# An adaLN block with linear attention and a SiLU MLP: EPS on ACT, mod products over four row tiles, other PSUM banks, engine orders drawn anew

## The chip, the cores and the metric

The kernel runs on one core of one Trainium2 chip. The metric is the device time of one execution in microseconds; the time of a kernel is the median of its timed runs. One further execution was taken by the hardware profiler, and all rows of the profile come from that one. TensorE is called PE here, VectorE DVE, ScalarE ACT, GpSimd POOL, and SP is the engine that issues most DMAs. L681 is line 681 of the kernel.

## The reference, cut to what matters

Sequence 2048, width D = 576, 32 heads of 18, hidden width F = 4608, all in fp32.

```
mod = (silu(c) @ w_mod).reshape(1, 6, 1, 576)
sa, ca, ga, sb, cb, gb = (mod[:, i] for i in range(6))
h = layernorm(x) * (1 + ca) + sa
q, k, v = heads(h @ wqkv);  phi(t) = where(t > 0, t + 1, exp(t)) + 1e-6
kv  = einsum("bhsd,bhse->bhde", phi(k), v);  z = einsum("bhsd->bhd", phi(k))
num = einsum("bhqd,bhde->bhqe", phi(q), kv)
den = einsum("bhqd,bhd->bhq", phi(q), z)[..., None] + 1e-6
x = x + ga * (merge(num / den) @ wo)
h = layernorm(x) * (1 + cb) + sb
x = x + gb * (silu(h @ w1) @ w2)
```

## The kernel before

**Arithmetic.** Each fp32 operand of a large product is split into a high part of type float32r and a low part that holds the rest (ACT copies the high part, DVE or POOL subtracts it: L118 and L311 for the low parts, L313 for the low part of a last chunk of 64 rows), and three products hi·hi, hi·lo and lo·hi are added in PSUM. So ACT and DVE have an eviction and a split to do for nearly everything that PE makes.

**Stages.** Tokens stand in 16 row tiles of 128, in four blocks of 512. First comes the start (0 to about 35 us): the column sums of the modulation for the first LayerNorm, statistics of the first four tiles (L175, L176), normalised tiles turned by PE (L383), modulated (L198) and split (hT, L118), and the first two k projections by passes (L400), each evicted by phi (L322 on ACT, L327 and L328 on DVE). Between those passes PE runs small products of constants that keep it occupied ("warm-ups", L405). Then a loop over t = 0 to 15 makes for each row tile a k projection (tile of PSUM psK), a v projection with its copies into vx, the kv product of the tile before (kv_mm, three PSUM tiles kvp0 to kvp2 that accumulate over all tiles) and one or two q projections. Between t = 5 and t = 8 the loop also makes the other four rows of the modulation: mod_piece (weights times silu(c), L511 and L513 on DVE, which wait for loads of w_mod), mod_row (L527, a row broadcast to all partitions, copied by ACT in L528) and mod_col (L520, columns for the second LayerNorm, copied by DVE in L522).

Then the masked kv matrix times wo is made per chunk (L706, split by L306 and L311/L313), beside q_norm of the first tiles. q_norm (L676 to L688) takes phi(q)·z, reduces it per head (L680), adds EPS (L681), inverts (L683) and multiplies (L684 on POOL); it then issues the load of x for the residual (L687, SP). The attention steps follow: s from 0 to 17 with three phases a step, q_norm of tile s, transposes of tile s − 1 (L738, with qT as the split result), the output product of tile s − 2 (L223 with qT, added in L752) and its LayerNorm statistics. Between the phases stand the late q projections (their PSUM comes from `big`, not psK), the turning of the second LayerNorm's tiles (L196, L211) and MLP group 0, made in the plain way (L812 up, L814 silu, L823 down, L828 add); its weights come by L768 and L770 (times gb) and are split in L771 and the line behind.

The other MLP groups (units, from about 380 us) use a scheme with seven products in place of eight per block: sums of blocks of h and of the weights (POOL's L955, L957, L960 and L1066, DVE's L933; sums of h go to DRAM and are streamed back into `room`), split by ACT (L936, L992, L1010) and DVE, up products L1248 with evictions (L1223 copies one to p, L1264, L1267) and down products L1321, added by DVE in L1329.

**PSUM.** The first pool holds kvp0 to kvp2 (a bank each), psK (two tiles of two banks) and psT (a bank). It is released after the loop and the M products; the second pool has three `big` tiles of two banks and two `small` ones of a bank. The pools give out banks in the order in which tiles are first asked for: before the change kvp0 to kvp2 are banks 0 to 2, psK 3 to 6 and psT 7, and `big` then covers 0-1, 2-3 and 4-5.

**Order.** Five engines have a fixed order for all that is issued before the first two units are done (about 405 us): the dictionary ORDERS holds for PE, DVE, ACT, POOL and SP a list of positions, and arrange (L104) chains the instructions of each engine in that order. An instruction thus waits for all that stands ahead of it on its engine, whatever it needs itself. What follows (units[2:], L1481) stands in program order on each engine and is interleaved by written-out plans.

The lines that the change touches outside the tables are the warm-ups' tile and the psT tile (L419 to L424 and L443), the modulation at t = 5 and 8 (L625 to L632) and L681.

Of the kernel before, what the change touches and what calls it, by code (L numbers as in the profile page):

```python
# [11 lines left out]
AF = mybir.ActivationFunctionType  # L12
# [6 lines left out]
EPS = 1e-6  # L19
# [3 lines left out]
def kernel(ctx: ExitStack, tc, A_x, A_wqkv, A_wo, B_x, B_w1, B_w2, c, w_mod, out):  # L23
# [28 lines left out]
    def f32(ap):  # L52
# [4 lines left out]
            0-107 114-116 108-110 117 111-113 118-2761  # L57
        """,
        "DVE": """
            1-2 0 6 4-5 11 7 12 8 13-14 9 18 15-16 10 17 19-20 29 21-22 24 23 25 28 26-27 30 45 31 46 32 34-35 37-38  # L60
            36 39-40 43 33 41-42 49 44 47-48 52 50-51 64 3 65 53-54 67 55 90 59 57 68 89 66 60 86 61 82 58 87 69 83
            88 62-63 84 70 150 73 71 74 72 75-76 91 78 77 56 80 85 81 93 79 94 92 151 95 152-153 99 98 100 96 154 97
            101-105 155 106-107 109 108 110-113 127-128 130 129 131 133-134 132 114 136 135 137-139 115 140-141 116
            143 117 144 142 118-126 145-149 156 184-186 157 187 160 188 161 225 189 162 158 224 164 159 163 228
            226-227 165 167 166 168-169 171 170 172-173 175 174 194-195 197 196 198-201 203-204 202 205-206 176
            207-208 210 177-179 209 211 180-183 190-193 212-216 218 217 219-220 222 221 223 229-230 232 231 233-261
            265 263 267-268 264 266 262 271-273 277-279 270 274-275 269 276 284 280-281 302 285 301 286 293 282
            294-295 305-307 287 303 314 288 315 289-291 283 304 316 324 292 325 296-299 326 308 300 333 309 334
            310-312 335 317 343 318 344 319-322 345 355 323 356 328-331 313 327 357 367 336 332 337 368 338-341 369
            376 342 377 348-349 346 350 353 351-352 347 378 387-388 358 354 359-366 389 406-407 370-371 375 408 425  # L70
            372-373 426 379-380 384 374 381-382 385 383 392 427 390 386 393 434 395 400 396-397 399 394 402 398 412
            435 413-414 403 415 391 416 422 411 417 421 420 418-419 401 436 405 428 423 409 424 410 429-432 404 433
            437-440 442-443 441 444-451 456 452-455 458-460 457 461-462 466 464 463 465 475 477 467 474 480 468-469
            482 478 471 486 483 473 472 489 470 488 496 495 494 479 484 476 497 491 485 490 498 481 487 506 499 501
            500 502 492 504 493 503 505 511 540 512 514 507-510 522 521 513 525 517 515-516 518-520 529 538 534
            523-524 526-527 539 528 531-532 530 533 535-537 542 541 543-546
        """,
        "Activation": """
            0-2 4-5 3 6-9 11 10 15 12 17 13-14 16 19 24 18 25 22 20 23 27 21 26 29 28 56 31 33 30 35 53 36-37 57 40
            34 54-55 38 41-42 39 48 32 43 49 51-52 50 58 44 46 59 47 45 60 62-65 67 66 61 68-72 74-75 73 76 79 77 80  # L80
            78 81-82 92 90-91 83-84 93 85-89 94-99 101-103 106 104 107 105 100 108-111 113-114 112 115 118 116 119
            117 120 131 121 129 132 130 122-128 133-136 138-139 137 140 143 141 144 142 145-147 149-150 148 151 154
# [13 lines left out]
        """,  # L96
        "SP": """
            0-27 31 34 28 30 32 35 33 29 42 36-37 43-46 51-53 38-41 54-57 59 58 60 47-50 67 66 65 61-62 68 63-64
            69-73 76 74-75 77-79 86 82 80-81 88 84 83 89 87 85 90-91 93 92 94 96 95 110 109 97 108 98-99 102 100
            103-104 101 105-107 114 111-113  # L100
        """,
    }
# [1414 lines left out]
```

## Time and profile before

| what | value |
|---|---|
| median of three timed runs | 1158.06 us (1158.06, 1159.26, 1156.38) |
| profiled execution | 1155.35 us, of which the span 1153.4 us |
| mean granted clock of PE | 0.996 |
| busy: PE / DVE / ACT / POOL | 1137.2 / 981.1 / 531.9 / 644.5 us |
| PE idle in the span | 16.2 us |
| DMA | 268.60 MB, 233 GB/s over the span |

The span is what the profiler's records cover; the 1.95 us beside it are start and end of the execution. A view of stretches gives the busy time of each engine in each stretch of the span and the clock that PE was granted, 1.00 being full speed. The view of waits sums how long an engine was idle ahead of an instruction, and names what ended the idleness. A timeline row has start, duration, engine, line, result and operands, and in brackets the idle time before it with what ended it. A releaser is inferred: what stands in brackets came last, not necessarily alone.

### The profile page before, as it was taken

What the parts mean: (1) busy time and instruction counts of PE and PEld (TensorE: products, weight loads), DVE (VectorE), ACT (ScalarE), POOL (GpSimd) and SP (SyncE); (2) the same over time, 40 slices, a digit from 0 to 9 for tenths busy, and PEclk for the clock granted to TensorE, in tenths of its full rate; (3) what the DMA queues carried; (4) which work ended last, traced back from release to release, by engine and by line L of the source; (5) the groups of instructions that cost most, each with busy time, mean ns of one, the idle gap of its engine ahead of it and who ended that gap; (6) DMA issues with size and microseconds to landing.
All of it is one profiled execution on the core that took longest, in us unless ns stands there. A gap on an engine that the chain in (4) does not pass through costs nothing.

```text
span 1153.4 us, 19610 instructions
## 1 busy us (share of the span) xinstructions
PE 1137.2 (99%) x7227; PEld 1056.4 (92%) x7227; DVE 981.1 (85%) x1554; ACT 531.9 (46%) x1085; POOL 644.5 (56%) x742
## 2 busy tenths in 40 slices
PE   8999999999999999999999999999999999999998
PEld 8999999899998899999999999999999999999998
DVE  6965644587788889998999999999999999999996
ACT  5643442436656544444444454454444444444541
POOL 1100000354533675777677667757767776776686
PEclk8999999999999999999999999999999999999999
DMA  9522100123158868769779769678697797697684
GB/s 288 155 82 78 42 1 1 45 72 124 33 230 311 311 262 332 300 249 349 275 260 355 276 255 360 267 295 326 261 340 291 256 349 277 256 356 277 254 311 154
DMA packets 58478, 268.60 MB, mean 233 GB/s; under 512 B 5580, under 2 KB 21712, under 8 KB 35344
## 3 DMA queue, kind: packets, MB, share of 16 engines
q1 hardware_dynamic: 58372, 267.36, 62.9%
q8 instruction: 57, 0.93, 0.3%
q14 instruction: 37, 0.30, 0.1%
q10 hardware_dynamic: 12, 0.00, 0.0%
HBM read 250.56 MB, written 16.78 MB: 232 GB/s over the span
## 4 chain that ended last, share of the span: by engine, by line
PE 92%; DVE 4%; DMA 2%; ACT 1%; issue 1%; POOL 1%; SPq 0%; DVEq 0%; ACTq 0%; POOLq 0%
PE up L1248 33%; PE down L1321 31%; PE psK L223 12%; PE big L223 5%; PE big L823 2%; PE small L812 2%; PE kvp L562 2%; PE small L211 1%; DMA room<-hd 1%; PE psK L706 1%; PE up L1351 1%; PE down L1351 1%; PE big L738 1%; PE psT L211 0%; DMA raw<-in_w_mod_dram 0%
## 5 line engine op out<-in xcount | busy, mean ns | idle before, releaser
L1329 DVE TENSOR_TENSOR acc<-down,acc 128x576 f32<-128x576 f32 x330 | 246.1, 753 | 12.6 <-PE down L1321 2.6
L1248 PE MATMUL up<-hT,w 128*128 128x512 f32 x916 | 239.5, 390 | 0.0
L1248 PEld LDWEIGHTS up<-hT,w 128*128 128x128 f32 x916 | 164.9, 189 | 24.8
L1283 POOL TENSOR_TENSOR s<-f,f 128x256 f32<-128x256 f32 x66 | 51.9, 786 | 160.4 <-ACT f L1264 160.4
L1321 PE MATMUL down<-w,hc 128*128 128x288 f32 x792 | 120.7, 294 | 0.0
L1321 PE MATMUL down<-w,hb 128*128 128x288 f32 x792 | 120.6, 294 | 0.0
L118 DVE TENSOR_TENSOR w<-v,w 128x288 fp32r<-128x288 f32 (+1 forms) x170 | 117.7, 700 | 1.9 <-ACT w L984 1.9
L1321 PEld LDWEIGHTS down<-w,hc 128*128 128x128 f32 x792 | 113.6, 188 | 5.3 <-DVE acc L1329 0.3
L1321 PEld LDWEIGHTS down<-w,hb 128*128 128x128 f32 x792 | 113.7, 188 | 5.1
L1329 DVE TENSOR_TENSOR U<-down,U 128x576 f32<-128x576 f32 x132 | 99.5, 754 | 16.4 <-PE down L1321 14.5
L223 PE MATMUL psK<-w,hT 128*128 128x288 f32 (+2 forms) x660 | 107.8, 298 | 0.5 <-POOL w L311 0.3
L223 PEld LDWEIGHTS psK<-w,hT 128*128 128x128 f32 x660 | 94.8, 189 | 1.3 <-POOL w L311 0.5
L1248 PE MATMUL up<-room,w 128*128 128x512 f32 x348 | 91.1, 390 | 0.1
L1302 POOL TENSOR_TENSOR hc<-s,hc 128x512 fp32r<-128x512 f32 x66 | 89.3, 1353 | 0.0
L181 POOL TENSOR_TENSOR rstd<-ve,neghalf 128x4 f32<-128x4 f32 (+3 forms) x10 | 9.3, 928 | 141.7 <-DVE ve L180 139.6
L1264 ACT ACTIVATE f<-f 128x512 f32<-128x512 f32 x102 | 64.4, 632 | 49.6 <-DVE f L1269 27.9
L1267 DVE TENSOR_TENSOR f<-up,p 128x512 f32<-128x512 f32 x102 | 69.7, 683 | 18.3 <-PE up L1248 15.5
L992 ACT CAST w<-v 128x288 fp32r<-128x288 f32 x85 | 36.7, 434 | 76.2 <-PE down L1321 62.3
L1248 PEld LDWEIGHTS up<-room,w 128*128 128x128 f32 x348 | 62.5, 188 | 9.8 <-DMA room<-hd 0.4
L1287 POOL TENSOR_TENSOR f<-f,s 128x256 f32<-128x256 f32 x66 | 51.1, 774 | 34.5 <-DVE hb L1302 22.9
L1321 PE MATMUL down<-w,he 128*128 128x288 f32 x396 | 63.0, 294 | 0.0
L1321 PE MATMUL down<-w,ha 128*128 128x288 f32 x396 | 63.0, 294 | 0.0
(285 smaller groups left out, 2534.4 us busy)
## 6 DMA issues: line engine op xcount, KB each, us to landing
hT<-hd SPq DMA_DIRECT2D x66, 1280.0 KB, 6.1
hT<-hd SPq DMA_DIRECT2D x45, 1024.0 KB, 5.2
room<-hd SPq DMA_DIRECT2D x35, 1280.0 KB, 6.0
room<-hd SPq DMA_DIRECT2D x20, 1024.0 KB, 5.5
v<-in_B_w_dram SPq DMA_DIRECT2D x17, 576.0 KB, 6.5
v<-in_B_w_dram SPq DMA_DIRECT2D x17, 512.0 KB, 7.7
hd<-S SPq DMA_DIRECT2D x6, 1024.0 KB, 3.9
xt<-in_A_x_dram SPq DMA_DIRECT2D x16, 288.0 KB, 3.7
```

The source lines that it names most:

```text
L118: return V.tensor_sub(lo, full, f32(hi))
L223: T.matmul(ps, xpart(a), wpart(b), start=n == 0, stop=n == len(XW) - 1)
L562: T.matmul(o, vt[:, j, h, :], pkt[:, :, j * HG : j * HG + P], start=(t == 0 and h == 0 and j % 2 == 0), stop=(t == NT - 1 and h == 1), ski ...
L992: A.copy(self.w2[n][:, 0], src)
L1248: T.matmul(ps, left, right, start=first and m == 0, stop=m == len(seq) - 1, skip_group_check=True)
L1264: A.activation(self.f[i, k], self.f[i, k], AF.Silu)
L1267: V.tensor_add(f, self.bank[bank[1]], self.p1)
L1283: G.tensor_add(self.s[:, 0:1], half(i, 0, 1), half(i, 1, 1))
L1287: G.tensor_sub(half(i, 1, 0), half(i, 1, 0), self.s[:, 1:2])
L1302: eng.tensor_sub(t[:, :, 1, :], src, f32(t[:, :, 0, :]))
L1321: T.matmul(ps[:, p, :HALF], self.a[i, n][:, u, p * P : (p + 1) * P], self.w.w2[n][:, v], start=n in (1, 5, 7, 6) and j == 0, stop=j == 2, ...
L1329: V.tensor_add(dst, ps[:, :, :HALF], dst)
```

## The change

1. In q_norm the addition of EPS to den moves from DVE (tensor_scalar) to ACT (activation, Identity with a bias tile). It is issued sixteen times.
2. The pieces of the modulation are made one row tile earlier (t = 4 and 7 in place of 5 and 8), and their four products, which stood in two pairs at the ends of t = 5 and t = 8, stand one each in t = 5, 6, 8 and 9, behind the v projection and ahead of the kv product.
3. The warm-ups write to kvp tiles, and psT is asked for ahead of psK. kvp0 to kvp2 stay banks 0 to 2, psT becomes 3 and psK 4 to 7. `big` then covers kvp0 with kvp1, kvp2 with psT, and the first psK tile; `small` takes the other.
4. The tables of all five engines are drawn anew. PE's becomes the program order; against the old one, four transposes of the start move behind the k products beside them.

The diff, without the tables but for PE's:

```diff
         "PE": """
-            0-107 114-116 108-110 117 111-113 118-2761
+            0-2761
         """,
...
-        warm_ps = ps2()
-        warm_up(8, warm_ps[:, 0])
         psc = psT()[:, : KC + 1]
+        warm_up(8, kvp[1][:, 0])
         T.transpose(psc, crow, ident[: KC + 1, : KC + 1])
-        warm_up(10, warm_ps[:, 0])
+        warm_up(10, kvp[1][:, 0])
...
-        warm_up(6, warm_ps[:, 0])
+        warm_up(6, kvp[2][:, 1])
         kps = [ps2() for _ in range(2)]
...
             if more and i >= 2:
                 turn(tb + 1, 3 * (i - 2) + 1)
+            if t == 5:
+                mod_row("ga", tm, 0)
+            elif t == 6:
+                mod_col(cols["b"], 0, tm[:, 1, :])
+            elif t == 8:
+                mod_col(cols["b"], 1, tm[:, 0, :])
+            elif t == 9:
+                mod_row("gb", tm, 1)
             if t > 0:
                 kv_mm(t - 1)
...
-            if t == 5:
-                tm = mod_piece(1)
-                mod_row("ga", tm, 0)
-                mod_col(cols["b"], 0, tm[:, 1, :])
-            if t == 8:
-                tm = mod_piece(2)
-                mod_col(cols["b"], 1, tm[:, 0, :])
-                mod_row("gb", tm, 1)
+            if t in (4, 7):
+                tm = mod_piece(t // 3)
...
             V.tensor_reduce(den, prod.rearrange("p (h d) -> p h d", d=DH), axis=AX.X, op=ALU.add)
-            V.tensor_scalar(den, den, EPS, None, op0=ALU.add)
+            A.activation(den, den, AF.Identity, bias=eps)
             r = const.tile([P, H], F32, name="r")
             V.reciprocal(r, den)
```

The new kernel's line numbers are 1 to 2 higher than the old one's. What the new tables do is shown at three places.

DVE at the start, from the modulation of a chunk (L198, later L199) on. hT is the low part of a turned tile, BN_STATS and BN_AGGR are the statistics of later row tiles. Before:

```order
L198 TENSOR_SCALAR raw<-kvp_109,col_a 128x256
L175 BN_STATS st<-xt 128x6 x4
L176 BN_AGGR mv<-st 128x2 x2
L180 TENSOR_SCALAR ve<-mv 128x2
L198 TENSOR_SCALAR raw<-kvp_108,col_a 128x256
L118 TENSOR_TENSOR hT<-raw,hT 128x256
```

After:

```order
L199 TENSOR_SCALAR raw<-kvp_109,col_a 128x256
L176 BN_STATS st<-xt 128x6
L119 TENSOR_TENSOR hT<-raw,hT 128x256
L176 BN_STATS st<-xt 128x6 x3
L177 BN_AGGR mv<-st 128x2 x2
L181 TENSOR_SCALAR ve<-mv 128x2
```

The low part of hT has moved ahead of three statistics, two aggregates and a modulation.

DVE at the attention's first output tiles, from the tile's weight load (L770, later L772) on. The w of the 128x2x576 row is the low part of MLP group 0's second weight; qT is the low part of the third output tile; the first L752 (L754) adds the first output tile. Before:

```order
L770 TENSOR_TENSOR raw<-raw,bc_gb 128x1152
L680 TENSOR_REDUCE den<-prod 128x32
L752 TENSOR_TENSOR acc_95<-big,acc_95 128x576
L681 TENSOR_SCALAR den<-den 128x32
L175 BN_STATS st<-acc_95 128x6 x2
L176 BN_AGGR mv<-st 128x2
L328 SCALAR_TENSOR_TENSOR acc_97<-e,acc_97 128x576
L118 TENSOR_TENSOR w<-raw,w 128x2x576
L683 RECIPROCAL r<-den 128x32
L680 TENSOR_REDUCE den<-prod 128x32
L328 SCALAR_TENSOR_TENSOR acc_98<-e,acc_98 128x576
L681 TENSOR_SCALAR den<-den 128x32
```

The row behind these is the low part of qT. After:

```order
L329 SCALAR_TENSOR_TENSOR acc_97<-e,acc_97 128x576
L682 TENSOR_REDUCE den<-prod 128x32
L754 TENSOR_TENSOR acc_95<-big,acc_95 128x576
L772 TENSOR_TENSOR raw<-raw,bc_gb 128x1152
L176 BN_STATS st<-acc_95 128x6 x2
L119 TENSOR_TENSOR w<-raw,w 128x2x576
L119 TENSOR_TENSOR qT<-big,qT 128x640
L685 RECIPROCAL r<-den 128x32
```

The low part of qT now follows the weight split at once; on the SP queue the load that L772 multiplies (L770 in the new numbering) stands behind two loads of x which it stood ahead of.

POOL and ACT at the first units. On POOL, v are weights of a later group and H is a sum of blocks of h. POOL before:

```order
L1086 TENSOR_TENSOR ht<-ht,sl 128x512
L933 TENSOR_TENSOR v<-v,bc_gb 128x288
L955 TENSOR_TENSOR v<-v 128x288
L1066 TENSOR_TENSOR H<-H,S 128x512
L933 TENSOR_TENSOR v<-v,bc_gb 128x288
```

POOL after:

```order
L1088 TENSOR_TENSOR ht<-ht,sl 128x512
L1067 TENSOR_TENSOR S<-S,H 128x512
L1068 TENSOR_TENSOR H<-H,S 128x512
L935 TENSOR_TENSOR v<-v,bc_gb 128x288
L957 TENSOR_TENSOR v<-v 128x288
```

The last sum H has moved ahead of the weight products. ACT before; S<-H are casts of that sum, wta a cast of weights, p the copy of an up product:

```order
L815 CAST hs<-sl 128x512
L795 CAST hT<-ht 128x512
L1010 CAST S<-H 128x512 x4
L936 CAST wta<-v 128x256
L1223 COPY p_4297<-up 128x512
```

ACT after:

```order
L816 ACTIVATE sl<-small 128x512
L817 CAST hs<-sl 128x512
L1012 CAST S<-H 128x512 x4
L1225 COPY p_4296<-up 128x512
L938 CAST wta<-v 128x256
```

The copy p has moved ahead of the cast wta.

71 lines of the change are left out of this document (36 added, 35 removed).

## The prediction

> **What bounds the kernel now.** I read the page first: the span and busy times, then the chain that ended last by engine. (In the timeline rows further down stand start, duration, engine, line, operation, result and operands; in brackets the idle time ahead and what ended it.)
>
> ```profile
> span 1153.4 us, 19610 instructions
> PE 1137.2 (99%) x7227; PEld 1056.4 (92%) x7227; DVE 981.1 (85%) x1554; ACT 531.9 (46%) x1085; POOL 644.5 (56%) x742
> PE 92%; DVE 4%; DMA 2%; ACT 1%; issue 1%; POOL 1%; SPq 0%; DVEq 0%; ACTq 0%; POOLq 0%
> ```
>
> TensorE is the bound. The change removes no matmul, so all that it can remove is PE's idle time, 1153.4 − 1137.2 = 16.2 us, and matmuls that run at a lowered clock. The stretches of the span come next (PE busy, PEld, DVE, ACT, POOL, granted clock, DMA share, GB/s).
>
> ```profile
> 240.00:260.00 20.00, 17.82 (x138) 17.61 (x137) 14.45 (x27) 5.59 (x9) 9.57 (x10) 1.00 0.15 45
> 380.00:400.00 20.00, 18.22 (x85) 15.17 (x85) 15.24 (x25) 10.70 (x24) 13.28 (x18) 0.91 0.83 305
> 440.00:1140.00 700.00, 699.87 (x4184) 638.95 (x4183) 657.09 (x963) 321.32 (x693) 509.06 (x592) 1.00 0.78 291
> ```
>
> From 440 to 1140 us PE lacks 0.13 us of 700 and has its full clock; there the program is the same before and after. What can change lies ahead of 405 us, where the tables hold, and two of these stretches lose 2.2 us (240 to 260) and 1.8 us (380 to 400) of PE. The waits of PE name the culprits (total us, times, longest).
>
> ```profile
> PE big L223 <- DVE qT L118: 2.2, 1, 2.2
> PE psK L400 <- DVE hT L118: 1.9, 1, 1.9
> PE up L1248 <- ACT p L1223: 1.8, 1, 1.8
> ...
> PE big L223 <- DVE v L313: 1.0, 1, 1.0
> ...
> PE psK L520 <- DVE acc L327: 0.6, 1, 0.6
> PE big L823 <- DVE hs L118: 0.6, 1, 0.6
> ...
> PE psK L706 <- DVE w L311: 0.3, 1, 0.3
> ```
>
> Each is one single wait at one place, and nearly all are for DVE or ACT work that stood behind other work in its engine's fixed order. So the question is, place by place, what stands ahead of it in the new order.
>
> **The change part by part.** *den on ACT.* The sixteen additions leave DVE.
>
> ```profile
> L681 DVE TENSOR_SCALAR den<-den 128x32 f32<-128x32 f32 x16 | 8.4, 527 | 0.2
> L683 DVE RECIPROCAL r<-den 128x32 f32<-128x32 f32 x16 | 5.6, 349 | 12.3 <-POOL pn L684 11.9
> L424 ACT ACTIVATE sc<-psT 128x5 f32<-128x5 f32 x1 | 0.2, 177 | 1.4 <-PE psT L422 1.4
> L325 ACT ACTIVATE acc<-acc,eps 128x576 f32<-128x576 f32 x7 | 5.5, 790 | 0.1
> ```
>
> DVE is rid of 16 × 0.527 = 8.4 us. On ACT no such operation is in the trace; its nearest rows are 0.177 us for 5 elements and 0.790 us for 576 with the same bias, which puts 32 elements at 0.177 + 0.613 × 27/571 = 0.21 us. Bounds: 0.18 and DVE's own mean 0.53, so 2.8 to 8.4 us on an ACT that is busy 5.59 of 20 us in the worst stretch. I take 0.21, 3.3 us in all, as the shape lies near the small row. The new hand-overs (DVE to ACT and back) fall in time that the reciprocal spends anyway: the sixteen wait 12.3 us, 11.9 of them for POOL's previous pn, 0.74 us each. By itself the edit is worth nothing except where DVE is late, as at 247 us below. Why the DVE form costs so much there is seen in its neighbour on POOL:
>
> ```profile
> 245.97 1.14 DVE L681 TENSOR_SCALAR den<-den 128x32 f32<-128x32 f32 x1
> ...
> 247.03 0.81 DVE L118 TENSOR_TENSOR qT<-big,qT 128x640 fp32r<-128x640 f32 x1
> ```
> ```profile
> 245.89 1.18 POOL L684 TENSOR_TENSOR pn<-acc,r 128x576 f32<-128x576 f32 x1 [1.46 <-PE big L738]
> ```
>
> The small addition lasts as long as POOL's product beside it: 245.97 + 1.14 = 247.11, and POOL ends at 247.07. [...]
>
> *The attention's first output tiles (220 to 260 us).*
>
> ```profile
> 245.10 0.71 PE L738 MATMUL big<-ident,pn 128*128 128x128 f32 x5
> 247.98 1.29 PE L223 MATMUL big<-w,qT 128*128 128x288 f32 x8 [2.18 <-DVE qT L118]
> ```
> ```profile
> 234.16 1.17 POOL L684 TENSOR_TENSOR pn<-acc,r 128x576 f32<-128x576 f32 x1 [0.64 <-DVE r L683]
> ```
> ```profile
> 236.41 1.88 DVE L770 TENSOR_TENSOR raw<-raw,bc_gb 128x1152 f32<-128x1152 f32 x1
> ...
> 242.01 2.32 DVE L118 TENSOR_TENSOR w<-raw,w 128x1152 fp32r<-128x1152 f32 x1
> ```
> ```profile
> raw<-in_B_w_dram SPq DMA_DIRECT2D x1, 576.0 KB, 3.7
> ```
>
> PE's 2.18 us end with the qT subtraction of 247.03. Ahead of it DVE did the weight split of 242.01 (2.32 us), a reciprocal, a reduce, q's last step and the slow addition: 5.02 us from 242.01 to 247.03. In the new order qT stands directly behind the split; the reciprocal, the reduce and q's step follow later, and the addition is gone. So qT starts 2.7 us earlier, 247.03 − 2.70 = 244.33 (242.01 + 2.32), even if nothing moves ahead of the split. The split itself can move up: three additions stood ahead of it since 231 us, 3 × 0.527 = 1.6 us by their mean, so qT may start at 242.7. PE, which saves the 1.3 us below, asks at 245.81 − 1.3 = 244.5. The wait goes: 2.2 us gained. Against it: the load for L770 now stands on SP's queue behind two x loads, the second of which needs the pn product of 234.16 to 235.33. That product waited 0.64 us for its reciprocal; without the additions it ends near 233, and 3.7 us later is 236.7, beside the 236.41 at which L770 starts now. If POOL is no earlier, the load lands at 235.33 + 3.7 = 239.0, L770 is 2.6 us later than now, that eats the 2.7 won, and the wait stays. Bounds 0 to 2.2, taken 2.2.
>
> PE's 1.0 us for v L313 ends because the late q projection's bank is another: after the release of the first pool its two banks are kvp2's and psT's, no longer half of the psK tile which L313 still reads. It now waits for L311 just ahead, done one DVE operation earlier. Gain 1.0, bounds 0 to 1.0. The 0.3 at L706 goes because w L311 moves ahead of one reduce-and-reciprocal step: gain 0.3. Together 3.5.
>
> *The first MLP units (380 to 400 us).*
>
> ```profile
> 385.98 2.62 PE L1248 MATMUL up<-xn,w 128*128 128x512 f32 x6 [1.78 <-ACT p L1223]
> ```
> ```profile
> 381.10 1.14 ACT L1010 CAST S<-H 128x512 fp32r<-128x512 f32 x2 [3.43 <-POOL H L1066]
> 385.04 0.41 ACT L936 CAST wta<-v 128x256 fp32r<-128x256 f32 x1 [2.80 <-issue]
> 385.35 0.58 ACT L1223 COPY p<-up 128x512 f32<-128x512 f32 x1
> ```
> ```profile
> 379.00 0.80 POOL L955 TENSOR_TENSOR v<-v 128x288 f32<-128x288 f32 x1 [5.88 <-DVE v L933]
> 379.76 1.30 POOL L1066 TENSOR_TENSOR H<-H,S 128x512 f32<-128x512 f32 x1
> ```
> ```profile
> 382.15 2.82 DVE L118 TENSOR_TENSOR S<-H,S 128x512 fp32r<-128x512 f32 x4
> ```
>
> This is a chain of orders. POOL's H sum stands behind a weight product that waits 5.88 us for DVE; ACT's casts of H wait 3.43 us for it; DVE subtracts after those (382.15 to 384.97); ACT's cast wta stands ahead of the copy p and is not let go until DVE is through; only then p frees what PE wants. After the change POOL does the H sum ahead of both weight products, ACT copies p ahead of wta, and one of the four subtractions stands earlier. Then p waits for its matmuls alone; those are over before 384.20 (385.98 − 1.78), so the 1.78 us go.
>
> The wait costs more than itself. Six matmuls take 2.62 us here, and the clock of the stretch is 0.91: 0.09 × 20 = 1.8 us of lost clock. Single microseconds show it (same columns):
>
> ```profile
> 247.00:248.00 1.00, 0.02 (x1) 0.05 (x1) 1.00 (x3) 0.00 (x0) 0.94 (x3) 1.00 0.00 0
> 387.00:388.00 1.00, 1.00 (x4) 0.72 (x4) 1.00 (x3) 0.44 (x1) 1.00 (x3) 0.50 0.81 266
> ```
>
> At 387 us the clock is halved, while the longer wait that ends at 247.98 leaves it at 1.00. [...] I count 1.5 of the 1.8 us as gained with the wait: 1.8 + 1.5 = 3.3, bounds 0 and 3.6.
>
> *The start (20 to 40 us).*
>
> ```profile
> 22.36 1.53 DVE L175 BATCH_NORM_STATS2 st<-xt 128x6 f32<-128x288 f32 x4
> ...
> 24.70 0.41 DVE L118 TENSOR_TENSOR hT<-raw,hT 128x256 fp32r<-128x256 f32 x1
> ...
> 29.34 0.76 DVE L327 TENSOR_SCALAR a<-psK 128x576 f32<-128x576 f32 x1 [0.16 <-ACT e L322]
> ...
> 34.05 0.76 DVE L327 TENSOR_SCALAR a<-psK 128x576 f32<-128x576 f32 x1
> ```
>
> The hT subtraction that PE awaits for 1.9 us moves ahead of three of the four statistics, so that wait nearly goes. But the same work still stands ahead of the eviction at 29.34, which had only 0.16 us to spare and frees the bank that PE needs next: DVE sets the pace here, and PE would wait there instead. The second eviction, at 34.05, gets two more statistics and an aggregate ahead, about 2 × 0.38 + 0.2 = 1.0 us later, with PE right behind it. I take −0.5, bounds −1.5 and +1.9.
>
> *mod products (96 to 145 us).* The row L520 that waited 0.6 us for the q eviction now follows v projections, with kv products behind it, so the 0.6 go; the two row products and two column products now stand at four places and use a psK tile between v and q each time, so that the q that follows asks for the bank of a copy. Between +0.6 and twice the 0.6 lost; I take +0.5, as DVE is idle for microseconds there.
>
> *The rest.* The hs wait of 0.6 us: DVE has less queued ahead, but ACT does casts ahead of hs; +0.5, bounds −0.6 and +0.6. The four transposes that PE puts behind the last k matmuls and the warm-ups' other banks are in front of work that waits for DVE anyway, so 0; uncovered, four transposes cost 4/5 of the 0.71 us that five take in the row of 245.10, 0.6 us.
>
> Sum: 3.5 + 3.3 − 0.5 + 0.5 + 0.5 = 7.3 us; for waits that a new order of five engines opens I take 0.3 off: 7.0. The profiled execution ran 1155.35 us, 1.95 outside its span; it would be 1148.35 with a span of 1146.4. It lies 2.7 below the median of the three timed runs, 1158.06, so the median forecast is 1158.06 − 7.0 = 1151.0.
>
> **The rivals.** *Given back.* The three large waits are replaced: L770's load late (the 2.2 stay), p released but PE then short of the next bank, the start at its worst (−1.5). With only a third of the 7.3 and the start's loss of a further 1.0, 1.4 us remain: 1157, within 0.3% (3.5 us, about what a measurement of this kernel can tell from no change). For it: DVE is 85% busy, so late work finds another victim. Against: each of the waits has its own cause in the order, and the causes are independent.
>
> *Start too.* If DVE's evictions at 29.34 also move up, the 1.9 us are gained and the −0.5 is not: 7.0 + 2.4 = 9.4, 1148.7.
>
> [...]
>
> *Slower.* One mechanism: DVE stands at each of the sixteen reciprocals until ACT has done the eviction step ahead of den (0.79, the row of L325) and den (0.21), 1.0 in place of 0.53, so 16 × 0.47 = 7.6 us more DVE time while the attention lasts, and PE follows. The qT gain of 3.5 goes with it, and 3.8 is left: 1158.06 − 3.8 + 7.6 = 1161.9. It decides from the point where ACT is over 0.74 us late on average, which is the reciprocals' present wait for POOL. Against it: that wait, and ACT's load of 5.59 of 20.
>
> **How the numbers follow.** Forecast 0.53, start too 0.10, clock 0.08, given back 0.19, slower 0.10. Of the first three, 0.71 in all, some 0.01 falls within 0.3%: faster 0.70, same 0.20, slower 0.10. The range takes in the first three with their bounds and most of the given-back case: 1147 to 1158, which leaves out the slower case and a tenth.
>
> **What would show it.** Right: in the profile after, no wait of PE for qT, for v L313 or for p; a granted clock of 1.00 from 380 to 400; PE at over 19.5 of 20 us in the stretches from 220 to 260; sixteen ACT additions near 0.21 us; the same DVE-bound waits at 25 to 36 us, about 2 us together. Wrong: PE waits of a microsecond in the first 405 us that are not in the list above; reciprocals that wait for ACT by more than 0.7 us each; the PE wait at 386 still there under another name; or a shift in the 700 us that both programs share.

## The result and the profile after

| what | before | after |
|---|---|---|
| median of six runs | 1156.32 us (1154.63 to 1159.26) | 1147.30 us (1146.04 to 1148.79) |
| profiled execution / span | 1155.35 / 1153.4 us | 1148.24 / 1146.3 us |
| PE busy / idle in the span | 1137.2 / 16.2 us | 1133.3 / 13.0 us |

The ratio is 0.992, with a 95% interval of 0.9903 to 0.9937: 9.0 us faster, 2.0 us more than the forecast gain of 7.0. Forecast was 1151.0 us, from 1147 to 1158, so 1147.3 lies only 0.3 us above the lower end; 1.7 of the 3.7 us between forecast and result come from before's own median, 1158.06 with three runs and 1156.32 with six. The two spans differ by 7.1 us (7.0 was forecast, 1146.4), 3.2 of it idle time of PE and 3.9 busy time; no matmul was removed, and the mean granted clock is 0.996 before and 1.000 after, so the latter is put down to the clock. The other 1.9 us lie in the choice of executions: before's profiled one is 1.0 below its median, after's 0.9 above.

The page of after, with the chain that ended last (busy and instructions of each engine, then shares of the chain):

```profile
span 1146.3 us, 19615 instructions
PE 1133.3 (99%) x7227; PEld 1053.7 (92%) x7227; DVE 971.2 (85%) x1538; ACT 534.6 (47%) x1101; POOL 648.3 (57%) x742
```

Still the same bound, PE at 99%; DVE has sixteen instructions and 9.9 us less, ACT 2.7 us more. The stretches of after, columns as before (PE, PEld, DVE, ACT, POOL, clock, DMA share, GB/s):

```profile
220.00:240.00 20.00, 18.90 (x125) 17.35 (x124) 13.87 (x21) 9.31 (x18) 11.31 (x12) 1.00 0.26 77
240.00:260.00 20.00, 20.00 (x156) 20.00 (x155) 15.88 (x30) 7.91 (x14) 11.98 (x12) 1.00 0.20 58
380.00:400.00 20.00, 19.92 (x106) 17.17 (x105) 15.39 (x28) 11.20 (x27) 17.01 (x23) 1.00 0.93 360
440.00:1140.00 700.00, 699.30 (x4187) 638.63 (x4186) 656.90 (x965) 317.35 (x685) 504.27 (x585) 1.00 0.77 290
```

The two bad stretches are full: 20.00 for 17.82 and 19.92 for 18.22, the second at clock 1.00 for 0.91. The long common part lost 0.6 us; with before's program there, b_act below gains 0.4 us on before and b_bank loses 0.6, so this is scatter. From 220 to 240 PE is busy for 18.90 us, short of the 19.5 that were forecast. The waits of PE in after name it:

```profile
PE psK L401 <- DVE hT L119: 2.0, 2, 1.0
PE kvp L406 <- DVE z L411: 1.2, 1, 1.2
PE big L224 <- DVE v L312: 1.1, 1, 1.1
PE psK L224 <- DVE col_b L522: 0.8, 1, 0.8
PE psT L384 <- ACT xt L189: 0.7, 1, 0.7
...
PE down L1353 <- DVE hb L1304: 0.5, 1, 0.5
```

No wait for qT or p is left, as forecast. The late q projection still waits, now 1.1 us for the chunk's low part L312 in place of 1.0 for the last chunk's L313.

To see where the time came from, the same matmul can be looked up in both traces. "Ahead" is its start in before less its start in after; the growth between two places is called a step.

| at, in before | 45 us | 90 | 185 | 226 | 248 | 348 | 368 | 388 | 408 | 1143 |
|---|---|---|---|---|---|---|---|---|---|---|
| after is ahead by | 0.90 us | 0.85 | 1.10 | 1.62 | 3.93 | 4.65 | 4.36 | 7.77 | 8.25 | 7.24 |

So the start gave 0.9, the mod products 0.25, the stretch from 220 to 260 us 2.8 (3.93 − 1.10), the part up to 348 us 0.7, the first units 3.6 net of a loss just ahead (8.25 − 4.65), and the rest took 1.0 back, half of it in the PE wait of 0.5 us for hb, which stands in the last 47 us and which before does not have. None of the seven kernels made from after (below), which run the same program there, has that wait either: it belongs to this execution, not to the change.

The rows behind the step at 248 us, DVE and then PE of after:

```profile
238.16 1.36 DVE L772 TENSOR_TENSOR raw<-raw,bc_gb 128x1152 f32<-128x1152 f32 x1 [1.29 <-DMA raw<-in_B_w_dram]
...
240.81 1.70 DVE L119 TENSOR_TENSOR w<-raw,w 128x1152 fp32r<-128x1152 f32 x1 [0.55 <-ACT w L773]
242.43 0.81 DVE L119 TENSOR_TENSOR qT<-big,qT 128x640 fp32r<-128x640 f32 x1
```
```profile
244.05 2.89 PE L224 MATMUL big<-w,qT 128*128 128x288 f32 x20
```

The load did come later, as the prediction feared: L772 waits 1.29 us for its DMA and starts at 238.16, where 236.41 was the time before and 236.7 the guess. But the split then takes 1.70 us for 2.32, qT follows at 242.43 and is through at 243.24 (242.43 + 0.81), 0.8 us ahead of PE's 244.05, which has no wait. At the first units, PE and ACT of after:

```profile
379.26 1.52 PE L1250 MATMUL up<-xn,w 128*128 128x512 f32 x6
```
```profile
378.10 0.59 ACT L1225 COPY p<-up 128x512 f32<-128x512 f32 x1 [3.78 <-PE up L1250]
378.62 0.41 ACT L938 CAST wta<-v 128x256 fp32r<-128x256 f32 x1
```

ACT is idle 3.78 us ahead of p, which waits for its matmuls alone, and the six matmuls that took 2.62 us take 1.52.

### The profile page after: what moved, and what is told of

Same layout as the page of the kernel before. It is cut to its first block, busy times and chain, and to the rows that moved or that the text cites. A ratio compares the mean times of both kernels' runs of the same rounds, so it can differ in the third digit from the quotient of the medians.

```text
span 1146.3 us, 19615 instructions
## 1 busy us (share of the span) xinstructions
PE 1133.3 (99%) x7227; PEld 1053.7 (92%) x7227; DVE 971.2 (85%) x1538; ACT 534.6 (47%) x1101; POOL 648.3 (57%) x742
## 4 chain that ended last, share of the span: by engine, by line
PE 90%; DVE 4%; DMA 3%; ACT 1%; issue 1%; POOL 0%; SPq 0%; POOLq 0%; DVEq 0%; ACTq 0%
PE up L1250 33%; PE down L1323 31%; PE psK L224 11%; PE big L224 6%; PE big L825 2%; PE kvp L562 1%; PE small L814 1%; DMA hT<-in_w_mod_dram 1%; DMA room<-hd 1%; PE psK L708 1%; DVE st L176 1%; DMA xt<-in_A_x_dram 1%; PE small L212 1%; PE up L1353 1%; DVE hT L119 1%
## 5 line engine op out<-in xcount | busy, mean ns | idle before, releaser
L1331 DVE TENSOR_TENSOR U<-down,U 128x576 f32<-128x576 f32 x132 | 99.5, 754 | 16.2 <-PE down L1323 14.1
```

The lines of the kernel that those rows point to most:

```text
L1331: V.tensor_add(dst, ps[:, :, :HALF], dst)
```

## The experiments

The prediction's theory was that each large wait has its own cause in the order of one or two engines, so that few rows carry the gain. The rivals: the waits hang on chains of rows, so that one row alone brings nothing; den on ACT is what relieves DVE; the banks or the spread of the mod products carry more than their terms. Names that begin with b_ are before with one part of the change, names with u_ are after with one part undone. The ratio is to before, timed beside it on the same chip; after's own is 0.992. The intervals are 3 to 5 us wide, and after was not timed again beside the others: of the kernels made from it, only u_mod lies clear of it by the ratios. What else is said of a single part rests on steps between two traces, one execution each.

### ACT's copy of p alone (b_act)

Before, with one ACT row moved:

```diff
 L1010 CAST S<-H 128x512 x4
+L1223 COPY p_4297<-up 128x512
 L936 CAST wta<-v 128x256
-L1223 COPY p_4297<-up 128x512
```

> The kernel before with one row moved: ACT copies p (L1223) ahead of the cast wta (L936). Theory A, one order each wait: wta alone held p back, since it is let go only when DVE's four subtractions of S end at 384.97; without it p follows the casts of 381.10 and its own up product, PE's 1.78 us at 386 go and the half clock behind them goes with them: 3.3 us less than before (3.0 to 3.6). Theory B, the chain of the prediction with POOL as its first link: the casts still wait 3.43 us for POOL, p still comes late, and 0 to 1 us is gained. Theory C, the gain came from DVE being relieved of the additions: 0.

Measured: 1153.20 us (1151.50 to 1158.91), ratio 0.9986 (0.9967 to 1.0004). Two stretches of it:

```profile
240.00:260.00 20.00, 17.83 (x125) 17.62 (x125) 13.72 (x26) 5.59 (x9) 8.46 (x9) 0.91 0.13 34
380.00:400.00 20.00, 19.63 (x100) 16.28 (x99) 17.30 (x28) 11.05 (x24) 16.97 (x21) 1.00 0.97 369
```

The p wait is gone, the clock there is 1.00, and against before's trace the step at this place is 3.7 us up to 391 us, of which 2.9 are left at 408 (in between PE waits 0.34 us for a load into `room`). POOL's row wasn't needed: the chain of the prediction, with POOL's sum first, falls, and ACT's row is enough. The median won 2.3 us, with an interval that still takes in no change. In the profiled execution the qT wait, the same 2.2 us as before, came with a lowered clock (0.91 for 1.00 in the first row), which cost 1.5 us that before's had not lost; whether that explains why the median is below theory A's 3.3 us was not shown.

### POOL's and ACT's rows undone in after (u_poolact)

POOL's sum H goes back behind the two weight products, and ACT's wta ahead of p:

```diff
 L1067 TENSOR_TENSOR S<-S,H 128x512
+L935 TENSOR_TENSOR v<-v,bc_gb 128x288
+L957 TENSOR_TENSOR v<-v 128x288
 L1068 TENSOR_TENSOR H<-H,S 128x512
-L935 TENSOR_TENSOR v<-v,bc_gb 128x288
-L957 TENSOR_TENSOR v<-v 128x288
...
+L938 CAST wta<-v 128x256
 L1225 COPY p_4296<-up 128x512
-L938 CAST wta<-v 128x256
```

> The kernel after with two rows of its tables put back: POOL's last sum of H behind the weight product that waits for DVE, and ACT's cast wta ahead of the copy p. Theory A and B alike: p is late again by the casts, the subtractions and wta, PE waits 1.0 to 1.8 us at the first units, and where the phase is bad the clock halves for another 1.5: 1 to 3.3 us more than after. Theory C: under 0.5 us more, since the additions are still on ACT.

Measured: 1147.00 us (1145.80 to 1149.59), ratio 0.9926 (0.9903 to 0.995). PE, then ACT:

```profile
379.69 1.66 PE L1250 MATMUL up<-xn,w 128*128 128x512 f32 x6 [0.34 <-ACT p L1225]
```
```profile
378.74 0.41 ACT L938 CAST wta<-v 128x256 fp32r<-128x256 f32 x1 [2.13 <-issue]
379.06 0.58 ACT L1225 COPY p<-up 128x512 f32<-128x512 f32 x1
```

Only 0.34 us of wait came back, with the clock at 1.00 from 360 to 400 us: a miss for every theory that made these two engines' rows the cause. wta is let go at 378.74, and p's copy can follow almost as soon as its matmuls are through, so something else in the new order covers the place. Theory C's number fits, and the next kernel tells the two apart.

### All three engines' rows undone (u_mlp3)

As u_poolact, and DVE's rows at the first units as before too: the four subtractions S in one piece, behind a sum of outputs (L830) that after does later.

```diff
-L119 TENSOR_TENSOR S<-H,S 128x512
 L830 TENSOR_TENSOR acc_98<-big,acc_98 128x576 x3
 L119 TENSOR_TENSOR hT<-ht,hT 64x512
-L119 TENSOR_TENSOR S<-H,S 128x512 x3
+L830 TENSOR_TENSOR acc_98<-big,acc_98 128x576
+L119 TENSOR_TENSOR S<-H,S 128x512 x4
 L119 TENSOR_TENSOR w<-raw,w 128x256
-L830 TENSOR_TENSOR acc_98<-big,acc_98 128x576
```

> The kernel after with all three orders of the first MLP units as before: POOL's last sum of H behind the weight product, ACT's wta ahead of p, and DVE's four subtractions of S behind the fourth addition of the plain down product. With the first two alone p came 0.34 us late in place of 1.78. Theory F, that DVE's rows covered for them: PE waits 1.5 to 1.9 us for p again, and 1.5 to 3.4 us more than after. Rival, that another row ahead of this place did it: under 0.5 us of wait.

Measured: 1148.35 us (1146.31 to 1148.56), ratio 0.9935 (0.9917 to 0.9953). Its first wait of PE:

```profile
PE up L1250 <- ACT p L1225: 1.4, 1, 1.4
```

The wait is back, with 1.4 us, and the clock is 1.00 from 360 to 400 us. So there are two cures for the place: ACT's order, which was enough in before (b_act), and DVE's one subtraction moved up and one sum moved back, which leaves 0.34 us in after (u_poolact). That goes against theory C, as the additions are on ACT here.

### qT's row alone (b_qt)

Before, with one DVE row moved:

```diff
 L118 TENSOR_TENSOR w<-raw,w 128x2x576
+L118 TENSOR_TENSOR qT<-big,qT 128x640
 L683 RECIPROCAL r<-den 128x32
 L680 TENSOR_REDUCE den<-prod 128x32
 L328 SCALAR_TENSOR_TENSOR acc_98<-e,acc_98 128x576
 L681 TENSOR_SCALAR den<-den 128x32
-L118 TENSOR_TENSOR qT<-big,qT 128x640
```

> The kernel before with one row of DVE's table moved: the third qT subtraction directly behind the weight split of 242.01, ahead of a reciprocal, a reduce, q's last step and the addition. Theory A: qT starts near 244.4 in place of 247.03, PE asks at 245.8, so the whole wait of 2.2 us goes and the time falls by 2.0 to 2.2. Rival: the reciprocal, now later, delays POOL's next pn and the transposes that need it, and half or more of it is given back: 0 to 1.1 less.

Measured: 1150.10 us (1149.51 to 1153.40), ratio 0.9965 (0.9952 to 0.9977).

```profile
240.00:260.00 20.00, 20.00 (x156) 20.00 (x155) 17.27 (x34) 6.29 (x10) 12.66 (x13) 1.00 0.18 49
380.00:400.00 20.00, 18.22 (x93) 15.33 (x92) 16.19 (x27) 11.48 (x26) 15.45 (x21) 1.00 0.92 337
```

The stretch is full, and the step there is 2.4 us, as much as after has at that place. In the second row the p wait of 1.8 us stands as before, PE is busy for the same 18.22 us, and yet the clock is 1.00 where it was 0.91; that gave this execution another step of 1.6 us, which no edit aimed at. It may not be this execution alone: the median won 4.6 us, twice theory A's 2.0 to 2.2, and six of the seven runs have a mean granted clock of 0.999, where before's eighteen beside them have 0.994 to 0.998. Why the clock stays up there is open. The rival falls: nothing was given back.

### Both rows together (b_two)

The edits of b_act and b_qt in one kernel, two rows of the whole change.

> The kernel before with both single rows moved at once: p ahead of wta on ACT, the third qT subtraction directly behind the weight split on DVE. Theory A, with the clock counted in: 2.2 us for qT and 1.8 for p, and the half clock that follows such a wait in some executions (1.5 us each, in about half of them) no longer occurs at either place: 5 to 6 us less than before, some 1149.5. Rival, DVE relief and the other rows are needed: under 3 us less.

Measured: 1150.70 us (1149.22 to 1151.98), ratio 0.9961 (0.9947 to 0.9975).

```profile
240.00:260.00 20.00, 20.00 (x157) 20.00 (x156) 17.37 (x34) 6.29 (x10) 12.32 (x13) 1.00 0.16 45
380.00:400.00 20.00, 20.00 (x104) 16.91 (x103) 17.95 (x30) 12.14 (x27) 17.10 (x22) 1.00 0.97 366
```

The steps are 2.4 and 3.4 us, and from 430 us on it is ahead of before by 6.0. By the medians it won 4.9 us (interval 2.9 to 6.1): two rows bring about half of the change's 9.0. But b_qt alone won 4.6 by the medians, so they don't show what the second row adds; that it adds 3.4 us here is seen in the trace. One would expect this if before pays for a lowered clock in one execution and not in another, which was not counted.

### den on ACT alone (b_den)

Before, with L681 as an activation, at the places in ACT's order where DVE's additions stood in time; of DVE's rows only the sixteen additions go.

```diff
-V.tensor_scalar(den, den, EPS, None, op0=ALU.add)
+A.activation(den, den, AF.Identity, bias=eps)
```

> The kernel before with the sixteen additions of EPS on ACT, each put into ACT's order where it stood in time on DVE; nothing else moved. Theory A: only the addition of 1.14 us in front of the third qT lies on the path, so PE's 2.2 us for qT become 1.1 to 1.3 and the time falls by 0.9 to 1.1 us. Theory C: 8.4 us off DVE are the larger part of the gain, 4 us or more less. The prediction's slower rival: reciprocals that wait for ACT, 4 us or more longer.

Measured: 1151.51 us (1149.75 to 1155.34), ratio 0.9974 (0.9956 to 0.9993). DVE of it:

```profile
233.62 0.35 DVE L683 RECIPROCAL r<-den 128x32 f32<-128x32 f32 x1 [0.93 <-ACT den L681]
...
238.96 1.35 DVE L118 TENSOR_TENSOR w<-raw,w 128x1152 fp32r<-128x1152 f32 x1
...
243.09 0.82 DVE L118 TENSOR_TENSOR qT<-big,qT 128x640 fp32r<-128x640 f32 x1
```

The whole qT wait is gone (step 2.4 us; 1.1 was expected), though the qT row stands where it stood: without the additions the split ahead of it starts at 238.96 for 242.01, of which 1.5 us are the lead that the whole trace has there from its start and 1.5 are won, and it takes 1.35 us for 2.32: 1.5 + 1.0 = 2.5. The p wait remains. So the qT wait too has two cures, each enough by itself in before. The median is 4.0 us less, which is theory C's number, but the trace does not bear it out: of its lead of 5.75 us at 408 us, 1.5 are from the start, 2.4 from qT and 1.7 from the clock at the p wait (1.00 this time); from 253 to 368 us, where eight of the sixteen additions stood, it gains 0.15. The price on DVE is small: the longest wait of a reciprocal for ACT is the 0.93 us above. (One of 3.67 us at 253.58, which the view puts down to ACT's qT, ends with POOL's pn at 252.38 + 1.17 = 253.55, as the same wait does in before.)

### The additions back on DVE in after (u_den)

Each of the sixteen as a DVE row directly ahead of its reciprocal, for instance:

```diff
 L119 TENSOR_TENSOR qT<-big,qT 128x640
+L683 TENSOR_SCALAR den<-den 128x32
 L685 RECIPROCAL r<-den 128x32
```

> The kernel after with the additions back on DVE, each directly ahead of its reciprocal; nothing else moved. Theory A: the new order has qT ahead of them with 0.8 us to spare, so 0 to 1 us more than after. Theory C: 4 us or more longer.

Measured: 1149.80 us (1147.61 to 1151.67), ratio 0.9949 (0.993 to 0.9968). Waits of PE that after does not have:

```profile
PE big L740 <- DVE den L683: 0.7, 1, 0.7
...
PE big L825 <- DVE hs L119: 0.5, 1, 0.5
```

Against after's trace it loses 0.9 us at 243 to 253 us, 0.35 at 304 to 314 and 0.7 at 324 to 334: 2.0 us in all, of the medians' 3.4 (0.29% of 1156): more than theory A's 0 to 1, less than theory C's 4. The other loss of its profile, 2.8 us by 61 us, lies at the start, which is the same program as after's; the clock was 0.79 there from 0 to 20 us.

### The banks (b_bank and u_bank)

In before the warm-ups go to kvp tiles and psT is asked for ahead of psK (b_bank); in after both go back (u_bank).

```diff
-        warm_ps = ps2()
-        warm_up(8, warm_ps[:, 0])
         psc = psT()[:, : KC + 1]
+        warm_up(8, kvp[1][:, 0])
```

> The kernel before with only the new banks: warm-ups in the kvp tiles, psT asked for ahead of psK. The prediction: PE's 1.0 us for v L313 falls away because the bank of the late q is another. Theory E, formed on the profile after: PE then waits for L311 of the same chunk, 0.97 us earlier at best, so the wait is nearly gone in this kernel (0.0 to 0.2 left), but DVE's qT subtraction does not come earlier and its wait grows from 2.2 to 3.1 us; no change, within 0.5 us. The prediction's own sum would give 1.0 us less.

Measured: 1155.94 us (1154.23 to 1159.33), ratio 1.0007 (0.9994 to 1.002). The waits of PE, and two stretches:

```profile
PE big L223 <- DVE qT L118: 2.2, 1, 2.2
...
PE big L223 <- DVE v L313: 1.0, 1, 1.0
```
```profile
240.00:260.00 20.00, 17.82 (x126) 17.61 (x125) 14.57 (x26) 5.25 (x8) 8.74 (x8) 0.91 0.11 31
380.00:400.00 20.00, 18.17 (x87) 15.12 (x86) 15.27 (x26) 8.80 (x20) 11.13 (x16) 0.91 0.84 305
```

The v wait stayed, to the tenth. The prediction's 1.0 us for the bank falls, and so does the expected 0 to 0.2 of wait. (qT's wait did not grow either.)

> The kernel after with the old banks (warm-ups in a psK tile, psK ahead of psT). If the banks carry a gain, the late q waits for the low part of the last chunk (L314, 228.51 in the profile after) in place of L312 (227.46): 1.0 us more than after, all of it on PE's path, since qT has 0.8 us to spare. If not, within 0.5 us of after.

Measured: 1148.65 us (1147.43 to 1149.49), ratio 0.9943 (0.9928 to 0.9959). Waits of PE that after does not have:

```profile
PE big L224 <- DVE v L314: 2.1, 1, 2.1
...
PE big L826 <- DVE acc L831: 0.7, 1, 0.7
```

In the new order L314 stands behind L312 and a reciprocal, and with the old banks PE waits 2.1 us for it, 1.0 more than after waits for L312 (step −1.1); it loses 0.7 us more at 126 to 145 us and 0.8 at 348 to 366, in all 2.3 us by 446 us. The 0.7 can't be put down to the banks: DVE waits there for a load of wo (L576 in after), and u_poolact, which has after's banks and program up to there, loses 1.0 us to after at the same place. Nor can the 0.8, which u_mod, with after's banks, loses too. What is left is 1.1 us.

The addresses in the built kernels say why. The late q takes the second `big` tile, and that lies in banks 4 and 5 in before, b_bank, after, u_bank and u_mod alike, not in 2 and 3 as the prediction took it. With the old banks (psK 3 to 6) it overlaps both psK tiles, so PE waits for the last chunk: L313 in before, L314 in u_bank. With the new ones (psK 4 to 7) it is just the first psK tile. In b_bank and u_mod the last chunk lies there (L313, L314), in after the chunk ahead of it (L312), since the spread mod products shift which of the two psK tiles comes next. So it takes the banks and the spread together.

### The mod products in two pairs again (u_mod)

```diff
-            if t == 5:
-                mod_row("ga", tm, 0)
-            elif t == 6:
-                mod_col(cols["b"], 0, tm[:, 1, :])
...
-            if t in (4, 7):
-                tm = mod_piece(t // 3)
+            if t == 5:
+                tm = mod_piece(1)
+                mod_row("ga", tm, 0)
+                mod_col(cols["b"], 0, tm[:, 1, :])
...
```

The other pair stands at t = 8 as in before. The evictions of the products move with them on DVE and ACT; DVE's rows that make the pieces keep their places in after's order.

> The kernel after with the products of the modulation back in two pairs at the ends of t = 5 and t = 8; the column evictions and the row copies of ACT and DVE stand behind the same neighbours as before. The prediction's term: the spread gained 0.5 us, so 0.5 us more. Rival 1: the four small waits that the pairs cause (0.6 and less) do not return in the new order, 0. Rival 2: the pair at t = 8 does without the 0.8 us that PE now waits for the column eviction behind three vx subtractions, 0.5 us less.

Measured: 1150.71 us (1147.25 to 1152.29), ratio 0.996 (0.9943 to 0.9977). The waits of PE:

```profile
PE big L224 <- DVE v L314: 2.1, 1, 2.1
PE psK L224 <- DVE mv L177: 1.7, 1, 1.7
...
PE psK L527 <- DVE col_b L522: 0.9, 1, 0.9
```

It loses 2.75 us between 90 and 155 us and 2.6 between 221 and 241, where PE waits 2.1 us for L314 as in u_bank, this time with a lowered clock (0.91 from 220 to 240 us); the banks above say why it is L314. All three expectations are missed. How much of the 2.75 us the spread carries is open: 1.7 us of it is PE's wait for mv L177, and that wait is 0.2 us in after and 1.2 in u_poolact, whose rows there are the same. Before, in two pairs, lost only 0.6 + 0.2 us to waits there, so the pairs cost more beside the new rows than beside the old.

### The start of DVE as before (u_startd)

After, with DVE's rows up to the 54th of the table as they stood; what PE awaits stands behind all four statistics again:

```diff
-L176 BN_STATS st<-xt 128x6
-L119 TENSOR_TENSOR hT<-raw,hT 128x256
-L176 BN_STATS st<-xt 128x6 x3
+L176 BN_STATS st<-xt 128x6 x4
```

> The kernel after with the first 54 rows of DVE (the start, to about 35 us) in the order of before. The prediction: DVE sets the pace there, so the order among its own operations hardly matters: PE's arrival at 45 us within 0.5 us of after where the clock is full in both. Rival: the early hT subtraction carried the 0.9 us by which the kernel after is ahead at 45 us, then 0.9 us more; the prediction's loss of 0.5 would give 0.5 us less.

Measured: 1148.34 us (1147.70 to 1149.90), ratio 0.9942 (0.9927 to 0.9957). The hT wait is one of 2.2 us in place of two of 1.0, the clock from 20 to 40 us is 0.91, and the lag on after's trace is 0.6 us at 61 us and 1.1 from 140 us on. In this pair of traces the rows make 0.5 us at 45 us with a lowered clock on one side, less than the start scatters by (below), so what they are worth is not settled; the 0.4 lost on the way to 140 us goes where DVE waits for the load of wo. That DVE sets the pace there, whichever way its rows stand, holds.

### A try for more (best2)

After, with the two waits that were left each given a row: v L312 ahead of a reduce that waits 1.3 us for POOL, and the second eviction of col_b ahead of the last two subtractions vx.

```diff
-L119 TENSOR_TENSOR vx_155<-psK,vx_155 128x2x126 x2
+L119 TENSOR_TENSOR vx_155<-psK,vx_155 128x2x126
+L522 TENSOR_SCALAR col_b<-psK 128x5
+L119 TENSOR_TENSOR vx_155<-psK,vx_155 128x2x126
...
+L312 TENSOR_TENSOR v<-psK,w 128x576
 L682 TENSOR_REDUCE den<-prod 128x32
-L312 TENSOR_TENSOR v<-psK,w 128x576
```

> The kernel after with two rows of DVE moved, against two waits that its profile shows: the low part of the wo product's v chunk (L312) ahead of the reduce that waits 1.3 us for POOL, and the second column eviction of the modulation (L522) ahead of the last two vx subtractions. PE's 1.1 us for v L312 fall to 0.2 to 0.5 and the 0.8 us for col_b to nothing: 1.3 to 1.7 us less than after. Rival: the reduce, now later, delays the second qT or the pn product, and half is given back.

Measured: 1148.65 us (1145.98 to 1152.75), ratio 0.9945 (0.9928 to 0.9962): not better than after. DVE, ACT and PE of it:

```profile
223.60 0.76 DVE L312 TENSOR_TENSOR v<-psK,w 128x576 fp32r<-128x576 f32 x1 [0.86 <-ACT w L307]
...
225.93 0.76 DVE L314 TENSOR_TENSOR v<-psK,v 64x576 fp32r<-64x576 f32 x1 [0.17 <-ACT v L307]
```
```profile
225.05 0.32 ACT L683 ACTIVATE den<-den,eps 128x32 f32<-128x32 f32 x1 [1.48 <-DVE den L682]
225.28 0.62 ACT L307 CAST v<-psK 128x576 fp32r<-128x576 f32 x1
```
```profile
226.75 3.99 PE L224 MATMUL big<-wq,hT 128*128 128x288 f32 x28 [2.34 <-DVE v L314]
```

The col_b wait is gone and gave 0.8 us there. But the row won at L312 was lost behind it: the reduce now stands behind v, so den comes later to ACT, where it stands ahead of the cast of the last chunk. ACT waits 1.48 us for the reduce, the cast L307 comes after, L314 after that, and PE waits 2.34 us for L314 in place of 1.10 for L312.

## Why the prediction was right, and where not

**The sum: right, with luck in it.** Span against span, 7.1 us came for 7.0. By the table the start brought 0.9 for −0.5, the mod products 0.25 for 0.5, 220 to 260 us 2.8 for 3.5, the rest 0.7 for 0.5, the first units 3.6 for 3.3, and 1.0 was lost for 0.3: what the start brought too much makes up for the bank and for a wait at the end.

**The two large waits: right.** 2.2 us for qT and 3.3 us for p with its clock were forecast; after's steps at the two places are 2.3 (1.62 to 3.93) and 3.4 to 3.9 (4.36 to 7.77 and 8.25), and b_two gets 2.4 and 3.4 from two rows. The working of the second was too long a chain: ACT's row cures it without POOL's (b_act), and DVE's without both (u_poolact against u_mlp3).

**v L313, 1.0 us: wrong.** The failed step is "after the release of the first pool its two banks are kvp2's and psT's": the late q's tile lies in banks 4 and 5, a psK tile, and b_bank shows that the new banks alone take nothing away. In after PE does wait for the other row, L312, as forecast, thanks to the mod products' new places; but DVE's new order puts a reduce ahead of it which itself waits for POOL:

```profile
226.04 0.75 DVE L682 TENSOR_REDUCE den<-prod 128x32 f32<-128x576 f32 x1 [1.30 <-POOL prod L1124]
226.71 0.75 DVE L312 TENSOR_TENSOR v<-psK,w 128x576 fp32r<-128x576 f32 x1
```

So 220 to 260 us brought 2.8 in place of 3.5.

**den on ACT: the price was low, the worth too.** The group of after:

```profile
L683 ACT ACTIVATE den<-den,eps 128x32 f32<-128x32 f32 x16 | 5.1, 320 | 15.3 <-DVE den L682 13.2 <-DVE st L176 2.1
L685 DVE RECIPROCAL r<-den 128x32 f32<-128x32 f32 x16 | 5.6, 347 | 14.1 <-POOL pn L686 13.7 <-ACT den L683 0.4
```

One takes 0.320 us, not 0.21, 5.1 us in all and not 3.3: the line drawn from 5 to 576 elements was off at its low end, whose row (0.177 us) shows no eps operand; whether that is why it is cheaper was not tried. The sixteen lie between 0.310 and 0.323 us in after, where DVE's sixteen in before lay between 0.17 and 1.43. The higher price did no harm: of the reciprocals' 14.1 us of waiting, 0.4 is for ACT, which also settles the slower rival, whose point was an ACT late by over 0.74 us each. But "by itself the edit is worth nothing except where DVE is late, as at 247 us" said too little: it removes that whole wait alone (b_den), and in after 2.0 us hang on it at three places, in one pair of traces (u_den).

**Mod products +0.5: half of it.** The 0.25 of the table are 1.4 us won up to 126 us and 1.1 given back by 155, of which 0.8 is a new wait for col_b. **The rest +0.5:** 0.7 up to 348 us; the hs wait is gone, as expected. The 0.3 taken off for new waits stands against 1.0 (8.25 to 7.24) of another kind: 0.7 of it is lost around the hb wait, which is this execution's own.

**The start, −0.5: not settled.** The reading that DVE sets the pace holds: after's waits from 22 to 35 us are 0.97, 0.99, 0.68 and 0.23 us, 2.9 together where about 2 were forecast; before's are 1.88, 0.31 and 0.30. After is 1.75 us ahead at 22 us and 0.9 at 45, so over the stretch that was forecast it loses 0.85; but b_qt, with before's start, goes from 1.8 to 0.4 there. The lead was won ahead of that. The first stretch of before and of after:

```profile
0.00:20.00 20.00, 17.63 (x107) 17.06 (x107) 12.07 (x31) 8.36 (x15) 4.08 (x13) 0.83 0.92 279
```
```profile
0.00:20.00 20.00, 17.99 (x122) 16.98 (x123) 12.19 (x34) 8.68 (x16) 4.03 (x13) 1.00 0.89 262
```

The clock differs, and the prediction gave that no term. How far a trace is ahead of before's near 61 us tells the scatter of one and the same start: 0, 1.2, 0.4, 1.6 and −0.3 us for before's start (before, b_act, b_qt, b_den, b_two), 0.85, 1.9, 1.5, 1.6, 2.05 and −2.0 for after's (after, u_poolact, u_mod, u_mlp3, best2, u_den). The medians are 0.4 and 1.5 us, a gain near 1.1 in place of −0.5, but either start scatters by 2 to 4 us. Nor does such a lead last: u_poolact's 1.0 us over after is gone at 128 us, since the load of wo lets DVE go on at 122.11 in both. The granted clock of 0 to 20 us was 1.00 in seven of the eight profiles whose start has after's PE and ACT rows (u_bank and u_startd among them), in one of the six with before's (b_act, where it is 0.92 from 20 to 40 us). Whether a row there does that, and which, was not tried and stays open.

**The rivals.** *Given back* and *slower* fall with the steps above. A clock that stays low, to which the chances give 0.08, did not happen in after's profile: no wait of more than 1.2 us is left in it, and the stretches quoted have 1.00. *Start too* gave 1148.7, nearest to the 1147.3 measured, but not by its mechanism, DVE's evictions earlier: PE still waits for DVE there.

## What to carry to other kernels

Where engines run fixed orders, first look for the one row that the bounding engine's wait names, and move that row alone: two rows were worth 4.9 of 9.0 us here by the medians. Undoing a part of a finished order does not price that part, since a second row may cover it (p, qT) or two parts work only together (banks, mod products); price a part both ways. And a row moved ahead of another moves the other back for everyone downstream, which is how the last try lost at L314 what it had won at L312.

## What the runs showed of the hardware

**A short wait lowered the clock in some executions and not in others.** The same wait at the same place, with the granted clock of its stretch: 2.2 us for qT, 1.00 in before, 0.91 in b_act and b_bank; 1.8 us for p, 0.91 in before and b_bank, 1.00 in b_qt and b_den. Four of seven have the lowered clock, which cost from 1.5 us (b_act) to 1.7 (before, by b_den's step) in these traces; in before it is 0.50 from 386.4 to 389.8 us, 3.4 us, and then 1.00 again. A wait of 2 us would thus cost about 2.9 on average here (2 + 4/7 × 1.6, an estimate from these rows). The wait's length does not decide alone: 1.8 us went with 0.91 in before, 2.2 us with 1.00. That a phase decides, as the expectation of u_poolact has it, is shown by no run.

**Some rows of DVE and POOL took longer side by side, the weight split too.** Before's sixteen additions took 0.17 to 1.43 us: 0.17 at 229.33, with POOL idle, 1.43 at 263.25, beside a product of POOL from 263.22 to 264.65, but also 0.17 at 260.65, where a product of POOL began with it. POOL beside the weight split, in before and in b_den:

```profile
241.62 1.50 POOL L684 TENSOR_TENSOR pn<-acc,r 128x576 f32<-128x576 f32 x1 [1.16 <-PE big L738]
243.19 1.25 POOL L686 COPY pn<-pn 128x64 f32<-128x64 f32 x1
```
```profile
240.11 1.22 POOL L684 TENSOR_TENSOR pn<-acc,r 128x576 f32<-128x576 f32 x1 [1.95 <-PE big L738]
241.40 0.24 POOL L686 COPY pn<-pn 128x64 f32<-128x64 f32 x1
```

In before the split runs from 242.01 to 244.33, with a product and a copy of POOL beside nearly all of it, and takes 2.32 us, and the copy of 64 columns 1.25. In b_den the product begins 0.2 us before the split ends (238.96 + 1.35 = 240.31): 1.35 us, and the copy 0.24. That would be why a row that left DVE earlier up made the split a microsecond shorter as well; that the work side by side is the cause is argued from these times, not shown by a run of its own.
